# A chunked retention recurrence with a soft mixture of experts: every product of the recurrence on 64x64 quadrants

## The chip, the core and the metric

The kernel runs on one core of a Trainium2 chip, in one launch. The metric is device time in microseconds (us). A core has a matrix engine (TensorE; in the profile PE for its matmuls and PEld for the loads of their stationary operand), a vector engine (DVE), an activation engine (ACT), a general engine (POOL) and a sequencer (SP) that here issues all DMAs. Matmuls write to PSUM, everything else lies in SBUF. All data is float32, and each float32 matmul of this kernel stands in the profile as two weight loads and two matmuls; a transpose on TensorE stands as one of each.

## The reference

```python
def _attn_ref(q, k, v):                      # each 4 x 8 x 768 x 64
    gamma = 1.0 - 2.0 ** (-5.0 - np.arange(H))
    state = zeros(B, H, D, D)
    for t in range(S):
        state = gamma * state + einsum('bhd,bhe->bhde', k[:, :, t], v[:, :, t])
        y[:, :, t] = D ** -0.5 * einsum('bhd,bhde->bhe', q[:, :, t], state)

def _moe_ref(x, phi, w1, w2):                # x 3072 x 512, 8 experts with 4 slots each
    logits = x @ phi                         # 3072 x 32
    d = softmax of logits over the tokens;  c = softmax of logits over the slots
    slot_input = d.T @ x
    for e in range(8):
        slot_out[e] = np.maximum(slot_input[e] @ w1[e], 0) @ w2[e]     # 512 -> 1024 -> 512
    return c @ slot_out
```

`x` is `y` with its heads side by side. `w1` and `w2` are 16.8 MB each; q, k and v 6.3 MB each.

## The kernel before

**Steps.** A batch of 768 tokens is cut into 6 chunks of 128, so that 4 batches make 24 steps `i` (`NSTEP`). The powers of gamma are put into a scale of `v` (`load_v`, on POOL) and a scale of the result (`scale`, on DVE), so that in between the recurrence is a plain one. Eight heads are handled as four pairs `g` of two heads `r`; the head `r` of a pair lies on partitions `64r` to `64r+63`.

**One step, in the order of TensorE** (its order is the program's; the other engines are ordered by a planner):

- `scores(i + 1)`: for each pair, head and half of the chunk (`late`), k times q, 64 stationary columns on 64 rows, which is one quadrant of the array; 192 or 128 moving columns. The last 64 of these multiply with an identity that lies behind q in the tile, which gives k in its natural layout for the state (not in the last chunk of a batch). DVE multiplies all 128x128 products of a head with the mask (L205, giving `A`), ACT copies the natural k (L209).
- `inter(i)`: the state times q, on quadrants, 128 moving columns (L223), into `y`.
- every fourth step, one of three pieces of the mixture of experts for the four steps before: `logits_mm` (L277), `dispatch_p` (L310) and `dispatch_u` (L319).
- `intra(i)`: `v` times the masked `A`, all 128 rows, 64 stationary columns, 128 moving columns (L234). It also multiplies the quarter of `A` that the mask has set to zero.
- `scale(i)` on DVE reads `y` (L245).
- `state(i)`: natural k times v, all 128 rows, 64 stationary columns, 64 moving columns (L258), added up in PSUM; ACT copies it to `sst` (L260), which `inter(i + 1)` reads.
- `natural(i - 1)`: four 128x128 transposes (L266), which ACT copies (L267).

**After the 24 steps** come the last group's logits, the slot inputs, the first expert layer (`hidden`, L486), the second (L578), and the combination with `c` (L560), whose output goes to memory in twelve DMAs of 512 KB.

**DMA.** SP issues everything, in one queue. A ring of 43 tiles of 4 KB a partition holds the weights (64 loads of 512 KB) and the working tiles of the recurrence (three a step). Within the 24 steps, 31/23 weight loads a step are issued ahead of `load_v(i + 2)` and `load_kq(i + 3)`; 7 more follow at the end (`TAIL`). k and q have four tiles in turn, so `load_kq(i + 3)` waits until step `i - 1` has read its own.

Of the kernel before, what the change touches and what calls it, by code (L numbers as in the profile page):

```python
# [17 lines left out]
C = 128  # L18
# [6 lines left out]
NE = 8  # L25
# [23 lines left out]
K_MASK, K_VSC, K_YT, K_FIRST = 0, 256, 304, 400  # L49
K_ID, K_YB, K_J, K_ALL = 400, 528, 552, 556  # L50
# [8 lines left out]
def half_of(r, g):  # L59


    return r if g < NPAIR // 2 else 1 - r


def head_of(half, g):
    return 2 * g + np.where(g < NPAIR // 2, half, 1 - half)


def constants():
    g = 1.0 - 2.0 ** (-5.0 - np.arange(H, dtype=np.float64))  # L70
    p = np.arange(128)
    k = np.zeros((128, K_ALL), np.float64)

    tok = np.stack([p, (p + D) % C], axis=1)
    k[:, K_MASK:K_MASK + 256] = (p[None, None, :] >= tok[:, :, None]).reshape(128, 256)
    t = np.arange(NC)[None, :, None] * C + tok[:, np.arange(H) // 2 % 2][:, None, :].astype(np.float64)
# [11 lines left out]
def retention_soft_moe_kernel(  # L88
# [15 lines left out]
    ring = ctx.enter_context(tc.tile_pool(name="ring", bufs=NRING))  # L104
    ps = ctx.enter_context(tc.tile_pool(name="ps", bufs=1, space=PSUM))
# [3 lines left out]
    def slot():  # L109
        return ring.tile([128, 1024], F32, name="r", tag="r")  # L110

# [18 lines left out]
    mask = kt[:, K_MASK:K_MASK + 256].rearrange("p (a t) -> p a t", t=C)  # L130
# [4 lines left out]
    w1t, w2t, w2n = {}, {}, [0]  # L135
    weights = [("w1", 4 * g + j, k) for g in range(2) for k in range(NK) for j in range(4)]
    for cb, (_, w) in enumerate(BLOCKS):
        for g in range(2):
            if w == 64:
                weights += [("w2", 4 * g + 2 * j, cb) for j in range(2)]  # L140
            else:
                weights += [("w2", 4 * g + j, cb) for _ in range(NFC // FPS[w]) for j in range(4)]

    def load_weights(n):
        for _ in range(n):
            if not weights:
                return
            which, e, k = weights.pop(0)
            t = slot()
            if which == "w1":  # L150
                nc.sync.dma_start(t, w1[e, k * 128:(k + 1) * 128, :])
                w1t[e, k] = t
            else:
                n = 1024 if BLOCKS[k][1] == 64 else FPS[BLOCKS[k][1]] * BLOCKS[k][1]
                nc.sync.dma_start(t[:, 0:n], w2[w2n[0]:w2n[0] + 128 * n].rearrange("(p n) -> p n", n=n))
                w2n[0] += 128 * n
                if BLOCKS[k][1] == 64:
                    w2t[e, k], w2t[e + 1, k] = [t[:, 0:512]], [t[:, 512:1024]]
                else:
                    w2t.setdefault((e, k), []).append(t)  # L160
# [19 lines left out]
    def load_v(i):  # L180
        t = slot()
        v = t[:, 0:512].rearrange("p (h e) -> p h e", e=D)
        st[i].update(v=v, kn=t[:, 512:1024].rearrange("p (h e) -> p h e", e=D))
        nc.sync.dma_start(t[:, 0:512], v_in[i])
        nc.gpsimd.tensor_tensor(v, v, vsc[:, i % NC, :].unsqueeze(2).broadcast_to([128, H, D]), ALU.mult)  # L185


    def scores(i):
        s = st[i]
        state = i % NC < NC - 1  # L190
        A = s["A"] = slot().rearrange("p (r g t) -> p r g t", r=2, t=C)
        for hf in range(2):
            scv = sct[hf][:, :, 0:384].rearrange("p r (g n) -> p r g n", n=192)
            for gg in range(2):
                g = 2 * hf + gg
                for late in range(2):
                    for r in range(2):
                        o = (late if g % 2 == 0 else 1 - late) * D
                        kb = KB[2 * g + late]
                        n = 2 + state - late  # L200
                        nc.tensor.matmul(scv[o:o + D, r, gg, late * D:(late + n) * D],  # L201
                                         s["kq"][r * D:(r + 1) * D, kb * D:(kb + 1) * D],
                                         blocks(s["kq"], r, NB - (2 - late) * QS[g], QS[g], n),
                                         start=True, stop=True)
            nc.vector.tensor_tensor(A[:, :, 2 * hf:2 * hf + 2], scv[:, :, :, 0:C],  # L205
                                    mask.unsqueeze(1).broadcast_to([128, 2, 2, C]), ALU.mult)
            if state:
                kn = s["kn"].rearrange("p (g r) e -> p r g e", r=2)[:, :, 2 * hf:2 * hf + 2]
                nc.scalar.copy(kn, scv[:, :, :, C:C + D])  # L209
# [3 lines left out]
    def inter(i):  # L213
        s = st[i]
        y = s["y"] = [ps.tile([128, 2, C], F32, name=f"y{b}") for b in range(2)]
        if i % NC == 0:
            return
        for gl in range(2):
            for b in range(2):
                g = 2 * b + gl  # L220
                for r in range(2):
                    o = half_of(r, g) * D
                    nc.tensor.matmul(y[b][o:o + D, gl, :], sst[r * D:(r + 1) * D, g, :],  # L223
                                     blocks(s["kq"], r, NB - 2 * QS[g], QS[g], 2),
                                     start=(gl == 0), stop=False, skip_group_check=True)

    def intra(i):
        s = st[i]
        c = i % NC
        y = s["y"]  # L230
        for g in range(NPAIR):
            for r in range(2):
                o = half_of(r, g) * D
                nc.tensor.matmul(y[g // 2][o:o + D, g % 2, :], s["v"][:, 2 * g + r, :], s["A"][:, r, g, :],  # L234
                                 start=(c == 0 and g % 2 == 0), stop=True, skip_group_check=True)

    def scale(i):
        s = st[i]
        y = s["y"]
        c = i % NC  # L240
        x = slot()
        yT = s["yT"] = x[:, 0:512].rearrange("p (g t) -> p g t", t=C)
        s["xn"] = x[:, 512:1024]
        for g in range(NPAIR):
            nc.vector.scalar_tensor_tensor(yT[:, g, :], y[g // 2][:, g % 2, :], ybs[:, c, g:g + 1], ysc[:, g, :],  # L245
                                           ALU.mult, ALU.mult)

    def state(i):
        s = st[i]
        c = i % NC  # L250
        if c == NC - 1:
            return
        if c == 0:
            spsum[0] = ps.tile([128, NPAIR, D], F32, name="S")
        S_ = spsum[0]
        for g in range(NPAIR):
            for r in range(2):
                nc.tensor.matmul(S_[r * D:(r + 1) * D, g, :], s["kn"][:, 2 * g + r, :], s["v"][:, 2 * g + r, :],  # L258
                                 start=(c == 0 and g == 0), stop=True, skip_group_check=True)
        nc.scalar.copy(sst, S_)  # L260

    def natural(i):
        s = st[i]
        xp = ps.tile([128, DM], F32, name="misc")
        for g in range(NPAIR):
            nc.tensor.transpose(xp[:, g * 128:(g + 1) * 128], s["yT"][:, g, :], ident)  # L266
        (nc.vector.tensor_copy if i == NSTEP - 1 else nc.scalar.copy)(s["xn"], xp)  # L267
# [3 lines left out]
    def logits_mm(g, js):  # L271
        q = gs.setdefault(g, {})
        if "ltp" not in q:
            q["ltp"] = ps.tile([128, C], F32, name="misc") if g < NGRP - 1 else pe_[0].tile([128, C], F32, name="sm", bufs=2)
# [32 lines left out]
    def dispatch_p(g):  # L307
        q = gs[g]
        pp = ps.tile([128, 128], F32, name="misc") if g < NGRP - 1 else pe_[0].tile([128, 128], F32, name="sm", bufs=2)
# [340 lines left out]
```

## Time and profile before

| | |
|---|---|
| median of 3 runs | 171.19 us (170.9 to 173.21) |
| profiled execution: its time / its span | 172.56 us / 170.8 us |
| TensorE clock granted, mean | 0.975 |
| PE busy | 153.2 us, 2748 matmuls |
| DVE / ACT / POOL busy | 90.8 / 55.4 / 30.8 us |
| moved by DMA | 59.63 MB, 349 GB/s over the span |

The page gives the busy time of each engine, a picture of the span in 40 slices, the DMA queues, the chain of waits that ended last, and the costliest groups of instructions. Beside it the trace answers by stretch (busy time and number of instructions in a window), by group and in order of time. An engine's name with "ld", as in PEld, is the weight load of TensorE. "issue" in the chain is time in which an engine waited for nothing that the profile shows. The count of a window holds every instruction that lies in it in part.

### The profile page before, as it was taken

What the parts mean: (1) busy time and instruction counts of PE and PEld (TensorE: products, weight loads), DVE (VectorE), ACT (ScalarE), POOL (GpSimd) and SP (SyncE); (2) the same over time, 40 slices, a digit from 0 to 9 for tenths busy, and PEclk for the clock granted to TensorE, in tenths of its full rate; (3) what the DMA queues carried; (4) which work ended last, traced back from release to release, by engine and by line L of the source; (5) the groups of instructions that cost most, each with busy time, mean ns of one, the idle gap of its engine ahead of it and who ended that gap; (6) DMA issues with size and microseconds to landing.
All of it is one profiled execution on the core that took longest, in us unless ns stands there. A gap on an engine that the chain in (4) does not pass through costs nothing.

```text
span 170.8 us, 6449 instructions
## 1 busy us (share of the span) xinstructions
PE 153.2 (90%) x2748; PEld 111.0 (65%) x2748; DVE 90.8 (53%) x259; ACT 55.4 (32%) x138; POOL 30.8 (18%) x40
## 2 busy tenths in 40 slices
PE   8599996999999999999899999999999999998500
PEld 2299985778887888777668887876325466665300
DVE  1456657655686687655866589761031202653600
ACT  3114431444441544333533443343020200533300
POOL 0252222223132222222320314001300000000000
PEclk9969999999999999999999999999999999999985
DMA  5999999897999989999998898799899999999993
GB/s 190 330 404 408 405 377 343 308 378 235 386 336 351 364 321 364 343 340 337 378 355 288 271 403 317 253 338 368 291 345 421 411 406 411 407 409 410 417 419 129
DMA packets 18317, 59.63 MB, mean 349 GB/s; under 512 B 2032, under 2 KB 2416, under 8 KB 18288
## 3 DMA queue, kind: packets, MB, share of 16 engines
q1 hardware_dynamic: 18288, 59.21, 93.1%
q8 instruction: 22, 0.36, 0.8%
q14 instruction: 7, 0.06, 0.1%
HBM read 52.91 MB, written 6.29 MB: 347 GB/s over the span
## 4 chain that ended last, share of the span: by engine, by line
PE 76%; DMA 10%; DVE 4%; issue 3%; ACT 1%; SPq 1%; DVEq 0%
PE sc L201 16%; PE y L234 13%; PE misc L266 8%; PE sc L578 6%; DMA r<-in_w_dram 6%; PE y L223 5%; PE S L258 5%; PE y L486 4%; DMA kq<-in_kq_dram 4%; PE misc L277 3%; PE misc L319 3%; PE misc L486 2%; PE S L486 2%; DVE r L245 1%; PE sm L363 1%
## 5 line engine op out<-in xcount | busy, mean ns | idle before, releaser
L205 DVE TENSOR_TENSOR r<-sc,kt 128x512 f32<-128x512 f32 x48 | 31.3, 684 | 20.9 <-PE sc L201 17.4
L185 POOL TENSOR_TENSOR r<-r,kt 128x512 f32<-128x512 f32 x24 | 25.3, 1053 | 72.5 <-DMA r<-in_v_dram 60.8
L201 PE MATMUL sc<-kq 64*64 64x128 f32 (+2 forms) x768 | 31.4, 301 | 2.1 <-DMA kq<-in_kq_dram 1.9
L245 DVE SCALAR_TENSOR_TENSOR r<-y,kt,ysc 128x128 f32<-128x128 f32 x96 | 27.6, 344 | 4.0 <-PE y L234 3.6
L201 PEld LDWEIGHTS sc<-kq 64*64 64x64 f32 x768 | 25.1, 136 | 7.1 <-issue 3.0
L234 PE MATMUL y<-r 128*64 128x128 f32 x384 | 27.5, 283 | 0.5 <-issue 0.4
L234 PEld LDWEIGHTS y<-r 128*64 128x64 f32 x384 | 21.3, 139 | 8.4 <-issue 5.1
L209 ACT COPY r<-sc 128x256 f32<-128x256 f32 x40 | 14.9, 372 | 32.2 <-DVE r L205 32.2
L578 PE MATMUL sc<-r 128*32 128x128 f32 (+1 forms) x384 | 16.3, 311 | 0.8 <-DMA r<-in_w_dram 0.8
L266 PE MATMUL misc<-kt,r 128*128 128x128 f32 x96 | 15.6, 285 | 1.0 <-DVE lb L305 0.7
L267 ACT COPY r<-misc 128x512 f32<-128x512 f32 x23 | 13.5, 586 | 8.4 <-PE misc L266 6.9
L578 PEld LDWEIGHTS sc<-r 128*32 128x32 f32 x384 | 10.7, 109 | 7.1 <-issue 2.9
L258 PE MATMUL S<-r 128*64 128x64 f32 x320 | 13.4, 222 | 1.6 <-issue 1.6
L260 ACT COPY sst<-S 128x256 f32<-128x256 f32 x20 | 7.4, 372 | 19.9 <-PE S L258 19.8
L266 PEld LDWEIGHTS misc<-kt,r 128*128 128x128 f32 x96 | 10.1, 141 | 5.0 <-issue 2.1
L223 PE MATMUL y<-kq,sst 64*64 64x128 f32 x320 | 12.7, 270 | 0.0
L258 PEld LDWEIGHTS S<-r 128*64 128x64 f32 x320 | 12.3, 138 | 0.4 <-issue 0.4
L223 PEld LDWEIGHTS y<-kq,sst 64*64 64x64 f32 x320 | 10.3, 133 | 0.2 <-ACT sst L260 0.2
L486 PE MATMUL y<-r,siT 128*32 128x512 f32 x64 | 8.2, 597 | 0.0
L367 ACT CAST r<-sm 128x512 fp32r<-128x512 f32 x4 | 2.2, 587 | 13.9 <-PE sm L363 13.9
L277 PE MATMUL misc<-r,phis 128*32 128x128 f32 x160 | 5.4, 276 | 0.3 <-issue 0.3
L563 ACT COPY r<-misc 128x512 f32<-128x512 f32 x3 | 1.8, 590 | 11.4 <-PE misc L560 11.4
(114 smaller groups left out, 130.3 us busy)
## 6 DMA issues: line engine op xcount, KB each, us to landing
r<-in_w_dram SPq DMA_DIRECT2D x64, 512.0 KB, 7.5
kq<-in_kq_dram SPq DMA_DIRECT2D x20, 512.0 KB, 5.7
r<-in_v_dram SPq DMA_DIRECT2D x24, 256.0 KB, 7.1
out_dram<-r SPq DMA_DIRECT2D x12, 512.0 KB, 9.7
kq<-in_kq_dram SPq DMA_DIRECT2D x4, 544.0 KB, 6.6
kt<-in_consts_dram SPq DMA_DIRECT2D x1, 200.0 KB, 3.6
kt<-in_consts_dram SPq DMA_DIRECT2D x1, 78.0 KB, 5.9
phis<-in_phi_dram SPq DMA_DIRECT2D x1, 64.0 KB, 6.7
```

Source lines behind the costliest of these rows:

```text
L185: nc.gpsimd.tensor_tensor(v, v, vsc[:, i % NC, :].unsqueeze(2).broadcast_to([128, H, D]), ALU.mult)
L201: nc.tensor.matmul(scv[o:o + D, r, gg, late * D:(late + n) * D], s["kq"][r * D:(r + 1) * D, kb * D:(kb + 1) * D], blocks(s["kq"], r, NB - ...
L205: nc.vector.tensor_tensor(A[:, :, 2 * hf:2 * hf + 2], scv[:, :, :, 0:C], mask.unsqueeze(1).broadcast_to([128, 2, 2, C]), ALU.mult)
L209: nc.scalar.copy(kn, scv[:, :, :, C:C + D])
L223: nc.tensor.matmul(y[b][o:o + D, gl, :], sst[r * D:(r + 1) * D, g, :], blocks(s["kq"], r, NB - 2 * QS[g], QS[g], 2), start=(gl == 0), stop ...
L234: nc.tensor.matmul(y[g // 2][o:o + D, g % 2, :], s["v"][:, 2 * g + r, :], s["A"][:, r, g, :], start=(c == 0 and g % 2 == 0), stop=True, sk ...
L245: nc.vector.scalar_tensor_tensor(yT[:, g, :], y[g // 2][:, g % 2, :], ybs[:, c, g:g + 1], ysc[:, g, :], ALU.mult, ALU.mult)
L258: nc.tensor.matmul(S_[r * D:(r + 1) * D, g, :], s["kn"][:, 2 * g + r, :], s["v"][:, 2 * g + r, :], start=(c == 0 and g == 0), stop=True, s ...
L266: nc.tensor.transpose(xp[:, g * 128:(g + 1) * 128], s["yT"][:, g, :], ident)
L267: (nc.vector.tensor_copy if i == NSTEP - 1 else nc.scalar.copy)(s["xn"], xp)
L486: nc.tensor.matmul(hp[g][half][32 * j:32 * j + 32, :], siT[:, k, :], w1t[4 * g + j, k][:, half * 512:(half + 1) * 512], start=(k == 0), st ...
L578: nc.tensor.matmul(op[32 * j:32 * j + 32, :w], hT[fc // 4][:, fc % 4, 4 * g + j, :], t[:, f * w:(f + 1) * w], start=(g == 0 and fc == 0), ...
```

## The change

All products of the recurrence, `intra` and `state` too, are done on 64x64 quadrants. A head's 128x128 `A` becomes three 64x64 blocks: two triangles on the diagonal, masked with one 64x64 triangle, and a full block that needs no mask; the fourth, all zero, is neither made nor multiplied. `intra` thus has three matmuls of 64 columns a head instead of one of 128 over 128 rows, and `state` two of 64 rows instead of one of 128. DVE masks half as many elements; ACT copies the full block together with the natural k.

As one PSUM place is now added to from both row halves of the array, each of these is done in two rounds (`second`): `attend(i, 0)` holds the state's part and the first half of `intra`, `attend(i, 1)` the rest, and between them a small copy on DVE (`turn`) reads one column of `y`, so that the second round waits for the first. `emit` orders the matmuls of several lists so that each quadrant gets the same number of columns. A step is now: state of `i - 1` (second round), scores of `i + 1`, state of `i` (first round); `attend(i, 0)`; `turn`; a piece of the mixture of experts, if one is due; `natural(i - 1)`; `attend(i, 1)`; `scale(i)`.

The logits and the dispatch of the groups lie in columns of the score tiles that the scores do not use; `dispatch_u` writes four pieces of 128 columns where it wrote 512. The ring holds weights only (35 tiles), the recurrence works in 18 tiles of 2 KB a partition, and four weights are loaded as two halves into those. In the recurrence 35/21 weight loads a step are issued from step 2 on, then 4 (`TAIL`). In the tail the k/q tiles hold the hidden layer.

```diff
-TAIL = (2, 2, 1, 2)
+TAIL = (0, 2, 2, 0)
-NPRE = 31
+NPRE = 35
-NRING = 43
+NRING = 35
+NHALF = 18
+NSPLIT = 4
...
+def row_of(late, g):
+    return late if g < NPAIR // 2 else 1 - late
...
+    def emit(*lists):
+        at, todo = {}, []
+        for ls in lists:
+            for quadrant, n, fn in ls:
+                todo.append((at.get(quadrant, 0), len(todo), fn))
+                at[quadrant] = at.get(quadrant, 0) + n
+        for _, _, fn in sorted(todo, key=lambda x: x[:2]):
+            fn()
...
+    def scores_out(i):
...
+        n = (1 + state) * D
         for hf in range(2):
             scv = sct[hf][:, :, 0:384].rearrange("p r (g n) -> p r g n", n=192)
...
+            nc.vector.tensor_tensor(A[:, hf], scv[:, :, :, 0:D],
+                                    tri.unsqueeze(1).unsqueeze(1).broadcast_to([128, 2, 2, D]), ALU.mult)
+            nc.scalar.copy(Bs[hf][:, :, :, 0:n], scv[:, :, :, D:D + n])
...
+    yb = [ps.tile([128, 2, C], F32, name=f"y{b}") for b in range(2)]
+
+    def turn():
+        nc.vector.tensor_copy(small("turn", [128, 1]), yb[0][:, 1, C - 1:C])
+
+    def attend(i, second):
...
+        for g in (0, 1, 2, 3) if second else (1, 0, 3, 2):
+            for r in range(2):
+                o = half_of(r, g)
+                y = yb[g % 2][rows(o), g // 2, :]
+                first = bool(g < 2 and not second)
+                if not second and c > 0:
+                    ls.append(product(y, o, C, sst[rows(r), g, :], r, blocks(s["kq"], r, NB - 2 * QS[g], QS[g], 2),
+                                      start=first, stop=False))
+                    first = False
+                a = 1 - r if second else r
+                late = a == row_of(1, g)
+                A = s["A"][rows(a), g // 2, r, g % 2, :]
+                v = s["v"][rows(a), 2 * g + r, :]
+                if late:
+                    ls.append(product(y[:, D:C], o, D, v, a, A, start=first, stop=bool(second)))
+                else:
+                    ls.append(product(y[:, 0:D], o, D, v, a, A, start=first, stop=True))
+                    ls.append(product(y[:, D:C], o, D, v, a, s["B"][g // 2][rows(a), r, g % 2, 0:D],
+                                      start=False, stop=bool(second)))
+        return ls
...
+    def state(i, second):
...
         for g in range(NPAIR):
             for r in range(2):
+                a = 1 - r if second else r
+                late = a == row_of(1, g)
+                ls.append(product(spsum[0][rows(r), g, :], r, D,
+                                  s["B"][g // 2][rows(a), r, g % 2, (1 - late) * D:(2 - late) * D], a,
+                                  s["v"][rows(a), 2 * g + r, :], start=bool(c == 0 and not second and g == 0), stop=True))
+        if second:
+            ls.append(((1, 0), 0, lambda: nc.scalar.copy(sst, spsum[0])))
+        return ls
...
+        us = [sct[k // 2][:, k % 2, 384:512] for k in range(NK)]
...
+        for k, uk in enumerate(us):
+            for j in range(GRP):
+                nc.tensor.matmul(uk[32 * j:32 * j + 32, :], q["p"][:, 32 * j:32 * j + 32],
+                                 st[GRP * g + j]["xn"][:, k * n:(k + 1) * n],
+                                 start=True, stop=True, tile_position=(0, 32 * j))
...
+            emit(state(i - 1, 1) if i > 1 else [], [] if last else scores(i + 1), state(i, 0))
+            if not last:
+                scores_out(i + 1)
+            emit(attend(i, 0))
+            turn()
...
+        if i > 0:
+            natural(i - 1)
...
+        if i > 0:
+            emit(attend(i, 1))
+            scale(i)
```

More of the change, by code (lines that the diff above doesn't have):

```diff
@@ L138, in retention_soft_moe_kernel @@
         for g in range(2):
[L139 to L142, printed above, removed]
+            weights += [("w2", 4 * g + j, cb) for _ in range(NFC // FPS[w]) for j in range(4)]
     def load_weights(n):
@@ L190, in scores @@
         state = i % NC < NC - 1
-        A = s["A"] = slot().rearrange("p (r g t) -> p r g t", r=2, t=C)
+        ls = []
+        for g in range(NPAIR):
+            for late in range(2):
+                for r in range(2):
+                    o = row_of(late, g)
+                    kb = KB[2 * g + late]
+                    n = 2 + state - late
+                    out_ = sct[g // 2][rows(o), r, g % 2 * 192:g % 2 * 192 + n * D]
+                    ls.append(product(out_, o, n * D, s["kq"][rows(r), kb * D:(kb + 1) * D], r,
+                                      blocks(s["kq"], r, NB - (2 - late) * QS[g], QS[g], n), start=True, stop=True))
@@ L192, in scores @@
+        return ls
+    def scores_out(i):
+        s = st[i]
+        state = i % NC < NC - 1
+        A = s["A"] = half_tile().rearrange("p (f r g t) -> p f r g t", f=2, r=2, t=D)
+        Bs = s["B"] = [half_tile().rearrange("p (r g n) -> p r g n", r=2, n=2 * D) for _ in range(2)]
+        n = (1 + state) * D
         for hf in range(2):
             scv = sct[hf][:, :, 0:384].rearrange("p r (g n) -> p r g n", n=192)
[L194 to L209, printed above, removed]
-    spsum = {}
[L213 to L225, printed above, removed]
@@ new lines, in scale @@
+    def scale(i):
+        s = st[i]
+        c = i % NC
+        yT = s["yT"] = half_tile().rearrange("p (g t) -> p g t", t=C)
+        for g in (0, 2, 1, 3):
+            nc.vector.scalar_tensor_tensor(yT[:, g, :], yb[g % 2][:, g // 2, :], ybs[:, c, g:g + 1], ysc[:, g, :],
+                                           ALU.mult, ALU.mult)
+    def state(i, second):
+        s = st[i]
+        c = i % NC
+        ls = []
+        if c == NC - 1:
+            return ls
+        if c == 0 and not second:
+            spsum[0] = ps.tile([128, NPAIR, D], F32, name="S")
@@ L248, in state @@
[L248 to L260, printed above, removed]
+                a = 1 - r if second else r
@@ L316, in dispatch_u @@
         last = g == NGRP - 1
[L317 to L320 removed]
+        us = [sct[k // 2][:, k % 2, 384:512] for k in range(NK)]
+        if last:
+            u = ps.tile([128, DM], F32, name="y1")
+            us = [u]
+        n = DM // len(us)
+        for k, uk in enumerate(us):
[3 more added lines that the diff above has]
+                                 start=True, stop=True, tile_position=(0, 32 * j))
         if g == 0:
[L322 removed]
+            for hf in range(2):
+                nc.scalar.copy(acc[:, hf * 256:hf * 256 + 256].rearrange("p (r n) -> p r n", r=2), sct[hf][:, :, 384:512])
         elif last:
@@ L398, in retention_soft_moe_kernel @@
         g, ph = i // GRP, i % GRP
-        budget += NPRE / (NSTEP - 1)
-        load_weights(int(budget))
-        budget -= int(budget)
-        if not last:
-            scores(i + 1)
-        inter(i)
+        if i > 1:
+            budget += NPRE / (NSTEP - 3)
+        load_weights(int(budget + 1e-6))
+        budget -= int(budget + 1e-6)
+        if i == 0:
+            emit(state(0, 0))
+            emit(attend(0, 0))
+            turn()
+            emit(attend(0, 1), state(0, 1), scores(1))
+            scale(0)
+            scores_out(1)
+        else:
+            emit(state(i - 1, 1) if i > 1 else [], [] if last else scores(i + 1), state(i, 0))
+            if not last:
+                scores_out(i + 1)
+            emit(attend(i, 0))
+            turn()
         if i + 2 < NSTEP:
```

151 lines of the change are left out of this document (74 added, 77 removed).

## The prediction, made before the change was run

> **What bounds the kernel now.** First the page: its engines, its DMA queues, and the shares of the chain of waits.
>
> ```profile
> PE 153.2 (90%) x2748; PEld 111.0 (65%) x2748; DVE 90.8 (53%) x259; ACT 55.4 (32%) x138; POOL 30.8 (18%) x40
> q1 hardware_dynamic: 18288, 59.21, 93.1%
> q8 instruction: 22, 0.36, 0.8%
> PE 76%; DMA 10%; DVE 4%; issue 3%; ACT 1%; SPq 1%; DVEq 0%
> ```
>
> TensorE carries the chain, and the DMA engines are close behind. The third line is small and will matter: 22 transfers of instructions, 0.36 MB / 22 = 16 KB each. TensorE alone has 2748 + 2748 = 5496 instructions in the trace, 250 for each of the 22.
>
> Second, the busy time by stretch, for the recurrence and for what follows it (time and PE, PEld, DVE, ACT, POOL busy with their counts; granted clock, DMA share, GB/s):
>
> ```profile
> 8.39:110.19 101.80, 98.30 (x2057) 80.81 (x2057) 69.52 (x196) 39.87 (x105) 27.29 (x32) 0.98 0.95 345
> 110.19:170.80 60.61, 49.22 (x650) 27.98 (x649) 18.75 (x59) 13.52 (x30) 2.30 (x3) 0.96 0.95 370
> 130.00:160.00 30.00, 27.94 (x457) 17.09 (x446) 10.41 (x28) 6.66 (x12) 0.00 (x0) 1.00 1.03 410
> ```
>
> In the recurrence PE is busy 98.3 of 101.8 us; the tail of 60.6 us moves the rest of the weights and the output, at up to 410 GB/s, which I take for the full rate. The change is worth what it does to the 101.8 us.
>
> Third, one regular step in order of time (PE alone: start, length, group):
>
> ```profile
> 16.51 1.32 PE L201 MATMUL sc<-kq 64*64 64x192 f32 x32
> 17.64 0.62 PE L223 MATMUL y<-kq,sst 64*64 64x128 f32 x16
> 18.19 1.09 PE L234 MATMUL y<-r 128*64 128x128 f32 x16
> 19.12 0.63 PE L258 MATMUL S<-r 128*64 128x64 f32 x16
> 19.68 0.65 PE L266 MATMUL misc<-kt,r 128*128 128x128 f32 x4
> 20.27 0.38 PE L201 MATMUL sc<-kq 64*64 64x192 f32 x4
> ```
>
> From start to start: scores 1.13 us, state's part 0.55, `intra` 0.93, `state` 0.56, transposes 0.59, together 3.76 us, with 84 matmuls and as many weight loads: 168 instructions.
>
> Fourth, the chain in order of time, where it has no PE work:
>
> ```profile
> 23.04 0.23 PE S L258 x6
> 23.27 0.28 issue
> 23.55 0.56 PE S L258 x10
> ...
> 28.46 1.33 issue
> ...
> 73.43 0.15 issue
> ...
> 78.55 0.29 issue
> ...
> 84.84 0.45 issue
> ```
>
> The first, for one, stops in the middle of a run of like matmuls, where nothing is waited for. The stretches from one resumption to the next tell why:
>
> ```profile
> 23.54:29.77 6.23, 4.91 (x125) 4.17 (x126) 3.79 (x12) 1.42 (x4) 1.12 (x2) 1.00 0.97 351
> 73.57:78.83 5.26, 4.97 (x125) 4.32 (x125) 3.23 (x8) 1.76 (x5) 1.76 (x2) 1.00 0.95 365
> 78.83:85.28 6.45, 5.84 (x126) 4.83 (x126) 5.10 (x19) 2.54 (x9) 1.77 (x3) 1.00 0.99 359
> 92.03:97.22 5.19, 5.19 (x136) 4.42 (x128) 3.48 (x8) 2.45 (x6) 2.09 (x2) 1.00 0.76 215
> ```
>
> The first three hold 251, 250 and 252 instructions of TensorE, the number of one instruction transfer (with a few semaphore instructions it is 256). So TensorE stops because its next block of instructions has not come. As each of these stretches begins and ends with such a stop, its length is what a block takes to come when the one before is entered: 6.23, 5.26 and 6.45 us, mean 5.98, with the DMA engines at a share of 0.95 to 0.99. The old kernel uses a block in about 251 / 168 x 3.76 = 5.6 us, so it just gets by. In the fourth stretch, where the DMA share was 0.76, PE was never idle over 5.19 us: there a block took no longer than that.
>
> The Trainium skill, "Runtime: NRT & Kernel Launch", section "Instruction fetch mechanics", says that instructions come in blocks of 16 KiB, 256 instructions, the next page being fetched while the current one runs; with that the trace agrees (251, 250, 252). It also holds that fetching is hidden because the sequencer dispatches slower than blocks come; the five stops say otherwise. By that rule the result would be that of the first rival below.
>
> **The change part by part.**
>
> *Array time.* Scores stream (8 x 192 + 8 x 128) / 4 = 640 columns a quadrant in 1.13 us, 1.77 ns a column. New: scores with both `state` rounds, 640 + 256 = 896 columns, 1.59 us; `attend` first, 256 + 192 = 448, 0.79; second, 192, 0.34; transposes 0.59; one change of tiling more around them, priced at what the old change after the state's part costs (0.55 less 256 x 1.77 ns = 0.10). Sum 3.41 us against 3.76: 0.35 saved a step, 8.4 us in 24.
>
> *Instructions.* Here the change adds. The counts of the old groups:
>
> ```profile
> L234 PE MATMUL y<-r 128*64 128x128 f32 x384 | 27.5, 283 | 0.5 <-issue 0.4
> L258 PE MATMUL S<-r 128*64 128x64 f32 x320 | 13.4, 222 | 1.6 <-issue 1.6
> 104.80 1.06 PE L319 MATMUL misc<-r,p 128*32 128x512 f32 x8
> ```
>
> `intra` triples (+768), `state` doubles (+320), `dispatch_u` goes from 8 to 32 in each of five groups (+120): 1208 matmuls and as many loads, 2416 instructions. The recurrence had 2057 + 2057 = 4114; it gets 6530, or 6530 / 251 = 26.0 blocks instead of 16.4. A regular step has 132 pairs, 264 instructions, so at 3.41 us a block is used up in 3.2 us. No stretch above shows one coming that fast. So TensorE is paced by its instructions: one block lies ready, 25 are waited for.
>
> What does a block take then? Waiting should shrink with the DMA load. The recurrence moves k, q and v (20 x 512 + 4 x 544 + 24 x 256 KB), 0.34 MB of constants and 38 weights of 512 KB, 39 MB in all:
>
> ```profile
> r<-in_w_dram SPq DMA_DIRECT2D x64, 512.0 KB, 7.5
> kq<-in_kq_dram SPq DMA_DIRECT2D x20, 512.0 KB, 5.7
> r<-in_v_dram SPq DMA_DIRECT2D x24, 256.0 KB, 7.1
> kq<-in_kq_dram SPq DMA_DIRECT2D x4, 544.0 KB, 6.6
> ```
>
> Over some 130 us that is 300 GB/s, a share of 0.74 of 410. Upper end: 5.6 us, half way between the shortest and the mean under full load. Lower end: if all of the block time were waiting and shrank with the load, 5.98 x 0.74 / 0.97 = 4.5. I take 5.0, nearest to the fourth stretch with its share of 0.76. Then the recurrence ends at 8.4 + 25 x 5.0 = 133.4 us instead of 110.2: **23.2 us later**. The array's 8.4 us are inside that pace and bring nothing. At 4.5 it is +10.7, at 5.6 +38.2.
>
> *DVE and ACT*, priced by these rows:
>
> ```profile
> L205 DVE TENSOR_TENSOR r<-sc,kt 128x512 f32<-128x512 f32 x48 | 31.3, 684 | 20.9 <-PE sc L201 17.4
> L209 ACT COPY r<-sc 128x256 f32<-128x256 f32 x40 | 14.9, 372 | 32.2 <-DVE r L205 32.2
> L267 ACT COPY r<-misc 128x512 f32<-128x512 f32 x23 | 13.5, 586 | 8.4 <-PE misc L266 6.9
> L266 PE MATMUL misc<-kt,r 128*128 128x128 f32 x96 | 15.6, 285 | 1.0 <-DVE lb L305 0.7
> 142.34 0.42 DVE L541 COPY os<-sc 128x256 f32<-128x256 f32 x1 [5.36 <-PE sc L578]
> ```
>
> 48 masks of half the size fall from 684 to about 420 ns (-13 us of DVE). ACT's copies double in size: 40 x 0.586 + 8 x 0.372 = 26 us for 15. Neither engine comes near its step, so both count nothing.
>
> *New waits.* `turn` stands on DVE behind the masks of the next scores, with `scale` and the logits' reductions behind it; TensorE's second round waits for it. Its cover is `natural` (0.59 us), and it is a one-column copy: nothing while paced, and 0.1 to 0.3 us a step if the cover is gone. Logits and dispatch now share PSUM tiles with the scores, which then wait for the logits' readers; the like wait on the old shared tile cost 0.7 us in all (L305 in the L266 row), and goes. Taken as even, with 0 to 3 us as ends.
>
> *Weights.* 35/21 of 0.524 MB a step with k, q and v are 1.66 MB, 4.0 us at 410 GB/s: above the array's step but below the paced one (264 / 251 x 5.0 = 5.3 us), so this too is hidden; without the pacing it is the next limit. The four halved weights add four DMA issues. In both kernels 39 weights can lie in SBUF before the first expert layer, so the tail has the same 25 loads and the output to move: 60.6 us, taken unchanged (1.5 us either way for the doubled small DVE instructions and for halves that come late).
>
> *Sum.* Span 170.8 + 23.2 = 194.0. The profiled execution took 172.56 us in its own time, the median of the runs is 171.19; the difference put on the median gives 171.2 + 23.2 = **194.4 us**.
>
> **The rivals.** All hang on the time of a block; the change breaks even where 25 blocks take the old 101.8 us, 4.07 us each. Two per cent, about what a measurement tells from no change, is 3.4 us or 0.14 us a block.
>
> *Faster: blocks come in time.* If a block takes under about 3.9 us (or more than one is fetched ahead), the array decides: 171.2 - 8.4 = 162.8, and up to 2.5 less as the five stops (0.28 + 1.33 + 0.15 + 0.29 + 0.45) go. DMA allows it: the last v has 33 weights ahead of it, 36.6 MB, 89 us at 410 GB/s. For it speaks that waiting is partly DMA load; against it, that this same load would then be at 0.9 and more, where 5.26 was the shortest seen. 0.12, at 160 to 167.
>
> *No change: 3.94 to 4.2 us a block*, the saved load shortening the wait more than in proportion; 171. 0.08.
>
> *Array no cheaper.* That 64-column matmuls on quadrants cost as much as longer ones is spoken against by the step above (`state`: 16 of 64 columns in 0.56 us, `intra`: 16 of 128 in 0.93), and it would be inside the pace.
>
> **How the numbers follow.** Paced by instructions: 0.80, its own range 182 (4.5 us a block) to 209 (5.6). The range that holds 8 in 10 reaches down over the no-change case: 168 to 209; left out are the faster case and blocks over 5.6 us. Faster by over 2%: 0.12; within: 0.08; slower: 0.80.
>
> **What would show it.** If right: the recurrence ends near 133 us; the chain has "issue" at some 45 us (25 x 1.8) instead of 5 (3% of 170.8); about 250 instructions between its stops; instruction transfers go from 22 to about 31 or 32; the DMA share in the recurrence falls to about 0.75; ends of the tail are alike. If the array decides: few issue stops, steps of 3.4 us. It would be wrong if a block came much faster at a lower DMA load, and too low if the granted clock fell in the stops: at half clock a block lasts 6.4 us of array time.

## The result: 18 per cent slower

The kernel after took 202.2 us (median of 4 runs, 200.5 to 203.4), the kernel before 172.2 us beside it: a ratio of 1.176, 95% interval 1.161 to 1.192. The profiled execution of the kernel after took 202.39 us, with a span of 200.5 us. From the page of the kernel after: the busy times, the slices of the granted clock and of the DMA engines, the queues, and the chain's shares.

```profile
PE 160.2 (80%) x3956; PEld 119.4 (60%) x3956; DVE 85.8 (43%) x309; ACT 65.8 (33%) x147; POOL 30.6 (15%) x42
...
PEclk9999999999979969999999999999999999999985
DMA  6999999999969996965573723209319999999994
...
q1 hardware_dynamic: 18864, 59.11, 78.3%
q8 instruction: 31, 0.51, 1.1%
...
PE 35%; DVE 5%; DMA 5%; ACT 5%; issue 5%; DVEq 0%
```

TensorE has 3956 matmuls and as many weight loads, 1208 more of each, as counted ahead, and 31 transfers of instructions instead of 22. Its share of the chain fell from 76% to 35%; but this chain reaches back to 81.92 us only, so its shares can't be set beside those of before. The DMA row is not even: full in most of the first 18 slices, well below that in all but one of the next twelve, full again in the tail.

By stretch, with the columns as before. The recurrence ends where TensorE starts on the last logits, now at 138.47 us; the second and third rows are its two parts, the fourth is the tail:

```profile
8.39:138.47 130.08, 103.37 (x3258) 87.92 (x3258) 62.43 (x222) 50.21 (x115) 28.75 (x36) 0.97 0.77 284
15.45:89.54 74.09, 54.51 (x1653) 45.90 (x1652) 31.68 (x114) 26.63 (x61) 14.75 (x16) 0.95 0.96 367
89.54:138.47 48.93, 43.81 (x1435) 37.46 (x1435) 27.77 (x99) 21.02 (x49) 12.06 (x15) 1.00 0.45 142
138.47:200.50 62.03, 49.96 (x655) 28.19 (x649) 21.27 (x82) 13.18 (x30) 0.40 (x1) 0.95 0.85 333
```

The recurrence takes 28.3 us more (130.08 for 101.80), the tail 1.4 more. In the recurrence TensorE is idle for 130.08 - 103.37 = 26.7 us, where it was 3.5 us: 23.2 of the 28.3. Its busy time rises by the other 5.1 us.

Who ended TensorE's idle time in the recurrence of the kernel after (total, times, longest):

```profile
PE y L213 <- issue: 9.1, 7, 2.3
PE sc L213 <- issue: 6.1, 5, 2.4
PE sc L374 <- issue: 3.4, 1, 3.4
PE S L213 <- issue: 1.9, 4, 1.2
PE sc L213 <- ACT p L361: 1.4, 3, 0.6
PE sc L326 <- ACT h L245: 1.4, 3, 0.7
...
PE sc L326 <- issue: 0.6, 2, 0.4
```

The rows "issue" add up to 21.1 us, where the kernel before had 2.3; all others to 4.8 instead of 2.9. So the time went mostly where the forecast put it: TensorE waits for nothing but its next instructions. 20.6 of the 21.1 us lie in 17 stops, and in the trace each of these comes a multiple of 256 instructions after the first of them (semaphore instructions counted), and 1.1 to 1.6 us after the end of a transfer of instructions. Stretches from one stop to the next, or to the next block, each one block of 256 instructions (a few records are missing); the share of the DMA engines is the last column but one:

```profile
42.10:48.12 6.02, 4.00 (x128) 3.22 (x127) 1.70 (x6) 2.29 (x5) 1.57 (x2) 1.00 1.02 406
48.12:54.24 6.12, 3.67 (x128) 3.19 (x128) 1.71 (x6) 1.54 (x3) 1.04 (x1) 1.00 1.03 404
54.24:59.51 5.27, 5.27 (x125) 4.75 (x129) 1.51 (x5) 1.34 (x3) 0.56 (x1) 0.68 0.67 229
64.90:71.85 6.95, 3.32 (x127) 2.77 (x127) 2.06 (x7) 1.25 (x4) 1.04 (x1) 0.98 1.02 400
71.85:77.84 5.99, 5.58 (x126) 4.60 (x127) 2.86 (x8) 2.03 (x4) 1.04 (x1) 0.74 0.84 332
97.58:101.22 3.64, 3.37 (x128) 3.00 (x127) 1.94 (x8) 2.13 (x4) 1.04 (x1) 1.00 0.46 141
101.22:105.60 4.38, 3.81 (x128) 3.17 (x128) 1.84 (x7) 1.52 (x6) 1.04 (x1) 1.00 0.70 219
```

In the fourth row PE is busy for less than half of the 6.95 us that the block lasts. In the third and the fifth the granted clock is 0.68 and 0.74: after the two longest stops (2.4 and 3.4 us) the clock stood at half for 3.4 us each.

### The profile page after: what moved, and what is told of

It reads as the page before. It is cut to its first block, busy times and chain, and to the rows that moved or that the text cites. A ratio compares the mean times of both kernels' runs of the same rounds, so it can differ in the third digit from the quotient of the medians.

```text
span 200.5 us, 8905 instructions
## 1 busy us (share of the span) xinstructions
PE 160.2 (80%) x3956; PEld 119.4 (60%) x3956; DVE 85.8 (43%) x309; ACT 65.8 (33%) x147; POOL 30.6 (15%) x42
## 3 DMA queue, kind: packets, MB, share of 16 engines
HBM read 52.81 MB, written 6.29 MB: 295 GB/s over the span
## 4 chain that ended last, share of the span: by engine, by line
PE 35%; DVE 5%; DMA 5%; ACT 5%; issue 5%; DVEq 0%
PE sc L653 5%; DMA r<-in_w_dram 5%; PE sc L213 4%; PE y L213 4%; PE y L559 4%; PE misc L314 3%; ACT h L245 2%; PE misc L559 2%; PE S L559 2%; ACT h L316 2%; PE sc L374 2%; PE S L213 1%; DVE h L288 1%; PE sc L326 1%; PE sm L423 1%
## 5 line engine op out<-in xcount | busy, mean ns | idle before, releaser
L213 PE MATMUL sc<-kq 64*64 64x192 f32 (+2 forms) x768 | 43.2, 300 | 8.9 <-issue 6.1
L213 PE MATMUL y<-h 64*64 64x64 f32 x1152 | 36.5, 227 | 5.4 <-issue 5.0
L199 POOL TENSOR_TENSOR h<-h,kt 128x512 f32<-128x512 f32 x24 | 25.0, 1043 | 81.2 <-DMA h<-in_v_dram 64.7
L213 PEld LDWEIGHTS y<-h 64*64 64x64 f32 x1152 | 31.1, 137 | 9.4 <-issue 7.0
L288 DVE SCALAR_TENSOR_TENSOR h<-y,kt,ysc 128x128 f32<-128x128 f32 x96 | 27.4, 344 | 20.9 <-PE y L213 20.9
L245 ACT COPY h<-sc 128x512 f32<-128x512 f32 (+1 forms) x48 | 25.6, 550 | 29.8 <-DVE h L243 28.0
L213 PE MATMUL S<-h 64*64 64x64 f32 x640 | 28.8, 223 | 2.7 <-issue 1.9
L213 PEld LDWEIGHTS S<-h 64*64 64x64 f32 x640 | 25.0, 136 | 4.1 <-issue 2.4
L243 DVE TENSOR_TENSOR h<-sc,kt 128x256 f32<-128x256 f32 x48 | 19.8, 420 | 14.3 <-PE sc L213 12.8
L653 PE MATMUL sc<-r,kq 128*32 128x128 f32 (+1 forms) x352 | 16.3, 304 | 0.6 <-DMA r<-in_w_dram 0.6
```

Source lines behind the costliest of these rows:

```text
L213: return (row, o), n, lambda: nc.tensor.matmul(out_, lhsT, rhs, skip_group_check=True, **kw)
L243: nc.vector.tensor_tensor(A[:, hf], scv[:, :, :, 0:D], tri.unsqueeze(1).unsqueeze(1).broadcast_to([128, 2, 2, D]), ALU.mult)
L245: nc.scalar.copy(Bs[hf][:, :, :, 0:n], scv[:, :, :, D:D + n])
L288: nc.vector.scalar_tensor_tensor(yT[:, g, :], yb[g % 2][:, g // 2, :], ybs[:, c, g:g + 1], ysc[:, g, :], ALU.mult, ALU.mult)
L653: nc.tensor.matmul(op[32 * j:32 * j + 32, :w], hT[fc // 2][:, fc % 2, 4 * g + j, :], t[:, f * w:(f + 1) * w], start=(g == 0 and fc == 0), ...
```

## The experiments

In none of the kernels is a part of the computation left out. The runs called "no weights" (and the one that adds idle matmuls to that) load all expert weights after the recurrence, so their tails are long and only their recurrences are compared; the idle matmuls write values that the next matmul overwrites. The numbers for all of them, read in the traces as for the two kernels above (end of the recurrence; instruction blocks that TensorE used in it, counted from the first place where one block ends and the next begins, at 9 to 12 us; length of a block, which is the time of its fetch only where TensorE stops for it; TensorE's idle time put down to "issue", and to all else that the view of waits names):

| kernel | recurrence ends, us | blocks | us a block | idle: issue | idle: else |
|---|---|---|---|---|---|
| before | 110.2 | 16.0 | 6.12 | 2.3 | 2.9 |
| after | 138.5 | 25.3 | 5.10 | 21.1 | 4.8 |
| e1, after, no weights | 125.7 | 25.3 | 4.59 | 9.8 | 8.1 |
| e2, after, 264 to 232 instructions a step | 134.9 | 22.3 | 5.61 | 16.5 | 6.4 |
| e3, before, idle matmuls | 138.2 | 25.0 | 5.16 | 11.2 | 0.3 |
| e4, before, new memory | 110.8 | 16.0 | 6.29 | 4.2 | 1.3 |
| e5, after, loads in order | 138.6 | 25.3 | 5.10 | 20.6 | 4.0 |
| e6, e2 and no weights | 116.3 | 22.3 | 4.81 | 3.4 | 6.2 |
| e7, e6 with the old PSUM tile | 122.7 | 21.4 | 5.29 | 1.3 | 18.4 |
| e8, before, no weights | 104.7 | 16.0 | 5.90 | 0 | 3.1 |
| e9, e3 and no weights | 126.2 | 25.0 | 4.65 | 1.9 | 1.8 |
| e10, before, loads in order | 107.7 | 16.0 | 6.06 | 2.4 | 2.5 |

**Which half of the change does it: e3 and e4.** e3 gives the kernel before nearly as many more instructions as the change does (2304 for 2416), and nothing else of it:

```
# kernel before, in inter()
+        for n in range(24 // 4):
+            for b in range(2):
+                for r in range(2):
+                    o = half_of(r, 2 * b) * D
+                    nc.tensor.matmul(y[b][o:o + D, 0, 0:1], s["kq"][r * D:(r + 1) * D, 0:D],
+                                     s["kq"][r * D:(r + 1) * D, 0:1], start=True, stop=True, ...)
         if i % NC == 0:
             return
```

> The old kernel with 24 idle matmuls a step ahead of the state's part, one moving column each, on quadrants, into places of y that are overwritten: 48 loads and 48 matmuls a step, 2304 instructions in all, the number that the change adds (2416). Nothing else of the change. Theory: 9.2 blocks more, so the recurrence is paced by its blocks, 25.6 x 5 = 128 us instead of 101.8, and ends near 137 (130 to 143) with stops some 250 instructions apart; whole time about 198. Rival, the slowdown belongs to the quadrants and their new waits: only the array time of the idle matmuls is added, at most a quarter of 58 ns for each of the 48, 0.7 us a step: the recurrence ends at 127 or sooner.

Measured: 199.97 us in one run (span 198.1), recurrence end 138.2. That is the pace by instructions, and not the rival. A step without a stop shows what the idle matmuls cost the array itself:

```profile
17.05:21.51 4.46, 4.46 (x137) 4.05 (x133) 2.41 (x7) 1.70 (x4) 0.83 (x1) 1.00 0.89 299
```

4.46 us for 3.76, so some 24 x 0.70 = 16.8 of the 28.0 us are array work; the idle time at "issue" rises by 8.9 us (11.2 for 2.3). e3 shows that instructions that do almost nothing cost this much, but it is not a pure copy of the kernel after, which has less array work and more waiting.

e4 is the other half alone, the new working set in the kernel before:

```
-NPRE = 31
+NPRE = 35
-NRING = 43
+NRING = 35
+NHALF = 18
+NSPLIT = 4
...
-        t = slot()
-        v = t[:, 0:512].rearrange("p (h e) -> p h e", e=D)
+        t = half_tile()
+        v = st[i]["v"] = t.rearrange("p (h e) -> p h e", e=D)
```

> The other half of the change alone: products, waits and PSUM places of the old kernel, but the ring of 35 tiles for weights only, the working set in 18 tiles of 2 KB, four halved weights, the new pace of the loads and the hidden layer in the k/q tiles. Theory (instructions): TensorE's program is the old one, so it comes out like the old kernel, ratio 0.98 to 1.02; if weights are fetched earlier and faster, blocks come a little later and a few us are lost in the recurrence. Rival, the new ring and its pace cost the time (DMA full from 10 to 88 us): ratio above 1.10.

Measured: 174.8 us, ratio 1.013 (1.009 to 1.018), recurrence end 110.8. The memory is not what made the kernel slow; the recurrence on quadrants is.

**Is it the DMA load that makes a block slow: e1, e8, e9, e5.** e1 is the kernel after without weights beside the recurrence:

```
-TAIL = (0, 2, 2, 0)
+TAIL = (0, 0, 39, 0)
-ORDERED = {mybir.EngineType.PE}
-NPRE = 35
+ORDERED = {mybir.EngineType.PE, mybir.EngineType.SP}
+NPRE = 0
```

> The changed kernel with SP's DMAs in the order of the program and no weight load within the 24 steps; the 39 come after them. Only the end of the recurrence is read (138.5 us in the changed kernel); the whole gets longer, since the weights come late. Theory, TensorE waits for its blocks of instructions, and these wait behind the DMA load: all blocks come as in the lightly loaded second half of the changed kernel (about 11.5 blocks of 251 instructions in the 49.0 us from 89.54, 4.3 us each, the shortest 3.7): the recurrence ends at 9.6 + 25 x 4.1 = 112, between 105 and 117. Rival, the new waits (turn, shared PSUM tiles, DVE and ACT chains) cost it: they do not change, and the recurrence ends at 133 to 139.

Measured: recurrence end 125.7, between the two. Its rows, with the weights away and where they come in:

```profile
15.00:100.00 85.00, 75.41 (x2436) 63.97 (x2439) 46.10 (x168) 37.90 (x87) 19.15 (x21) 1.00 0.50 162
108.00:125.74 17.74, 12.85 (x410) 10.49 (x408) 9.28 (x35) 6.02 (x16) 2.77 (x5) 1.00 0.95 362
```

In 85 us TensorE used (2436 + 2439) / 256 = 19.0 blocks, 4.46 us each, at a DMA share of 0.50: blocks do come sooner. The theory gave too early an end for two reasons: a block still took 4.46 us where no weights moved, not 4.1 (9 us in 25 blocks), as other waits (8.1 us) showed under the stops; and the weights were issued from 109 us on, before the recurrence was over, and held up its last two steps. e8 and e9 close the second gap with a load that waits for the last step's k and q to be used, ahead of the weights:

```
+    nc.sync.dma_start(kqt[3][:, 0:1024], kq_in[NSTEP - 1, :, 0:1024])
     load_weights(TAIL[2])
```

> The old kernel with no weight load before the recurrence has ended. Theory: its stops (4.3 us in all at block boundaries) come from the DMA load, so they go, and nothing else changes: the recurrence ends at 104 to 107 instead of 110.2. Rival, a block takes its time whatever the DMA does: 109.5 to 111.

> The kernel before with 24 idle one-column matmuls a step (overwritten by what follows, so nothing is left out), and with all weights loaded only after the recurrence. In the run with idle matmuls and weights beside it, a regular step that met no stop took 4.46 us from transposes to transposes against 3.76 us in the kernel before, so the idle matmuls are 24 x 0.70 = 16.8 us of array work. Theory (a block of instructions comes sooner when the DMA engines have little to do): 216 instructions a step in 4.46 us use up 256 in 5.3 us, more than the 4.2 to 4.4 us that blocks took in the runs without weights, so the stops all but go (under 2 us in sum instead of 14.6) and the recurrence ends at 104.7 + 16.8 = 121.5 us (120 to 123). Rival (a block takes its 5.2 to 5.7 us whatever the load): 8.4 + 25 x 5.2 to 5.7 = 138 to 151 us, with stops as before.

e8: recurrence end 104.7, as the theory had it, with no idle time at "issue" at all, where the kernel before had 2.3 us. That is part of the 5.5 us by which it ends sooner; another 1.7 us is the clock, which stood at half for 3.41 us in the kernel before (first row) and not in e8, and no run shows that the weights caused that. e9: end 126.2, 4.7 us later than the 121.5 forecast and 3.2 past its range, but far from the rival's 138 and more. The idle at "issue" fell from e3's 11.2 to 1.9 us. Of the miss, 1.9 us are these stops, which the expectation allowed for (under 2) and did not add, and 1.7 are again 3.41 us at half clock (second row); the last 1.1 is open.

```profile
8.50:11.91 3.41, 3.41 (x44) 3.05 (x45) 1.44 (x3) 0.66 (x2) 2.19 (x5) 0.50 1.02 395
```

```profile
16.49:19.90 3.41, 3.41 (x44) 2.96 (x44) 1.20 (x4) 0.96 (x2) 0.92 (x1) 0.50 0.71 208
```

The recurrences as rows, e8, then e9, then e3:

```profile
8.39:104.71 96.32, 94.82 (x2057) 78.60 (x2049) 69.38 (x198) 40.01 (x105) 26.67 (x32) 1.00 0.56 183
```

```profile
8.39:126.22 117.83, 115.30 (x3209) 98.05 (x3209) 69.97 (x198) 40.03 (x105) 26.74 (x32) 0.99 0.46 152
```

```profile
8.39:138.24 129.85, 117.99 (x3198) 99.26 (x3189) 70.33 (x196) 40.11 (x105) 26.61 (x31) 0.97 0.79 272
```

e3 and e9 run the same instructions; the DMA share in the recurrence is 0.79 in the one and 0.46 in the other, and the recurrence 12 us shorter, 9.3 of them at "issue". e5 then asks whether it helps to spread the weights evenly:

```
-ORDERED = {mybir.EngineType.PE}
+ORDERED = {mybir.EngineType.PE, mybir.EngineType.SP}
```

> The changed kernel, with SP's DMAs in the order of the program, so that the weights come evenly (35/21 a step from step 2) instead of all before 88 us. Theory, a block of instructions waits behind the DMA queue: the same bytes spread over the recurrence; if the wait is proportional to the load, the mean block stays near 5.1 us and the recurrence ends at 135 to 141; if it grows faster than the load, it gets shorter, 126 to 134, and the whole 189 to 197. Rival, DMA load plays no part: 138 and 200 with no difference along the recurrence.

Measured: 202.85 us in one run, recurrence end 138.6 (138.5 in the kernel after). The load did become more even (first and second part of the recurrence: 0.82 and 0.73, for 0.96 and 0.45):

```profile
15.45:89.54 74.09, 59.59 (x1906) 50.35 (x1906) 35.77 (x129) 29.98 (x68) 14.69 (x16) 1.00 0.82 286
89.54:138.55 49.01, 39.76 (x1180) 33.80 (x1180) 23.14 (x85) 17.84 (x42) 9.90 (x13) 0.90 0.73 264
111.03:114.62 3.59, 3.59 (x137) 3.33 (x133) 2.57 (x8) 1.80 (x4) 1.04 (x1) 1.00 1.00 387
```

A block took 4.98 us in the first part and 5.32 in the second (3812 / 256 = 14.9 blocks and 2360 / 256 = 9.2), where the kernel after has 5.74 and 4.36: against that kernel the blocks moved with the load, and what the first part gained the second lost. (That e5's second part has the longer blocks at the lower share goes with its clock, 0.90 for 1.00: TensorE is idle for 1.0 us a block in both parts, and busy for 4.3 us a block instead of 4.0.) The end at 138.6 alone would fit the rival as well; what speaks against it is this shift along the recurrence. In this range the wait goes about in proportion to the load, and evening it out brings nothing. (The third row, a regular step without a stop, is used below.)

**What the wait depends on.** For the blocks of eight of these recurrences (before, after, e1 to e5, e9; the first of each left out) I counted in the trace how many bytes of loads had been issued and not yet begun to move when TensorE entered a block. The transfer that brings the next block begins 1.24 us after that, plus 1.38 us for each MB in waiting (171 blocks, correlation 0.87). Where TensorE then stops, the block's length is 2.55 us plus 0.96 times that delay (81 blocks, correlation 0.99):

| in waiting, MB | blocks with a stop | mean length, us |
|---|---|---|
| under 0.3 | 7 | 3.98 |
| 0.3 to 0.8 | 20 | 4.69 |
| 0.8 to 1.5 | 26 | 5.63 |
| over 1.5 | 28 | 6.35 |

Counted a few tenths of a microsecond earlier or later, the slope is 1.2 to 1.4 us a MB and the correlation 0.83 to 0.88. So a block's time goes with how much is queued when it is asked for. e5 fits: its mean in waiting is 0.84 MB a block, that of the kernel after 0.85. No run changed the queue alone, at the same load, so this is a relation read off the runs; that the load is a cause is what e1, e8 and e9 show.

**Fewer instructions: e2, a miss.** In the kernel after, the early half of each pair of blocks is multiplied in two matmuls of 64 columns; e2 lays their operands side by side and does it in one of 128:

```
-                    ls.append(product(y[:, 0:D], o, D, v, a, A, start=first, stop=True))
-                    ls.append(product(y[:, D:C], o, D, v, a, s["B"][g // 2][rows(a), r, g % 2, 0:D],
-                                      start=False, stop=bool(second)))
+                    ls.append(product(y, o, C, v, a, s["AB"][g // 2][rows(a), r, g % 2, 0:C],
+                                      start=first, stop=bool(second)))
```

> The changed kernel, with the triangle and the full block of the early half of a chunk side by side in SBUF, so that one matmul of 128 columns does what two of 64 did: 8 matmuls a step less (16 loads and 16 matmuls, 768 instructions in 24 steps), the same columns in the array, the same rounds and waits. One tile of the weight ring pays for the space (38 weights before the first expert layer instead of 39). Theory, paced by instructions: 768 / 251 = 3.06 blocks less at 4.9 us (130 us for 26) = 15 us less, 10 to 18; ratio to the old kernel about 1.09. Rival, the array or the new waits decide: no change beyond 2 us either way, ratio 1.17.

Measured: 200.8 us, ratio 1.165 (1.157 to 1.173), recurrence end 134.9: 3.6 us sooner where 15 were expected. Three blocks fewer, but each took longer:

```profile
15.00:91.00 76.00, 58.02 (x1526) 49.14 (x1525) 33.24 (x120) 28.53 (x65) 14.25 (x16) 0.93 0.96 361
91.00:134.91 43.91, 39.71 (x1179) 33.56 (x1179) 26.98 (x93) 18.74 (x44) 10.95 (x14) 1.00 0.46 147
```

In the first part 3051 instructions in 76.0 us are 6.38 us a block, against (1653 + 1652) / 256 = 12.9 blocks in 74.09, 5.74, in the kernel after, at the same DMA share of 0.96. My theory took the time of a block as given by the share. At its stops e2 had 1.65 MB in waiting, the kernel after 1.22; by the relation above (1.11 us a MB for the blocks with stops) that is 0.5 of the 0.8 us by which they differ there (6.22 and 5.41). Why its queue was longer I have not settled. In the second part few stops are left and other waits decide.

**What is under the stops: e6 and e7.** e6 is e2 and "no weights" with the gate; e7 puts logits and dispatch back into the PSUM tile of the kernel before:

```
-            q["ltp"] = sct[1][:, 1, 384:512] if g < NGRP - 1 else ...
+            q["ltp"] = ps.tile([128, C], F32, name="misc") if g < NGRP - 1 else ...
...
-        pp = sct[0][:, 0, 384:512] if g < NGRP - 1 else ...
+        pp = ps.tile([128, 128], F32, name="misc") if g < NGRP - 1 else ...
...
-        us = [sct[k // 2][:, k % 2, 384:512] for k in range(NK)]
+        u = ps.tile([128, DM], F32, name="y1" if last else "misc")
+        us = [u]
```

> No weight load before the recurrence has ended (they wait for a k/q tile that its last step reads), and the merged matmuls of e2: TensorE has 22.3 blocks to the end of the recurrence, and DMA carries k, q and v alone. Only the end of the recurrence is read. Theory A, blocks alone set the pace: 9.8 + 22.3 x 4.3 = 106, or sooner, as a step then uses a block in 3.7 us. Theory B, without the stops the new waits are next (steps of e1 without a stop: 3.8 us regular, 4.9 to 5.5 with a piece of the mixture of experts): four steps 18.5 us, the recurrence ends at 115 to 121.

> As e6, and logits, dispatch weights and dispatch products back in the PSUM tile that they had in the old kernel (shared with the transposes) instead of in the score tiles. Theory B, the sharing with the scores makes the new waits: the step after the logits falls from 5.2 to about 4.1 us and the recurrence ends 4 to 7 us sooner than in e6. Theory A: within 1 us of e6. If the transposes now wait for the logits' readers, as they did in the old kernel, up to 3 us of it come back.

e6: recurrence end 116.3, in the range of theory B. With few stops left (3.4 us) the new recurrence, here with the merged matmuls, still ends 11.6 us after the old one under the same condition (e8, 104.7). Step by step, from transposes to transposes, the five steps with a `dispatch_u` take 5.5 us longer than in e8, the other six up to 48 us, with most of the stops, 3.7, the last two 1.7, and the rest 0.7 together. Its stretch, and its largest waits on TensorE besides "issue":

```profile
8.39:116.33 107.94, 97.05 (x2855) 82.23 (x2850) 61.91 (x222) 49.92 (x115) 28.59 (x35) 1.00 0.51 163
```

```profile
PE sc L215 <- ACT p L364: 2.9, 5, 0.6
...
PE sc L329 <- ACT ab L249: 1.1, 2, 0.8
```

e7 is a miss on both sides: end 122.7, later instead of sooner. Where the waits went, and a regular step that met none:

```profile
L317 PE MATMUL misc<-kt,h 128*128 128x128 f32 x92 | 15.1, 286 | 12.6 <-DVE mrun L356 6.7 <-DVE acc L387 3.6 <-DVE lb L357 1.6
```

```profile
78.79:82.36 3.57, 3.57 (x117) 3.27 (x117) 1.98 (x6) 1.71 (x4) 0.78 (x1) 1.00 0.43 148
```

On the old tile the next transposes must wait for DVE to have read the logits and the dispatched sums: 12.6 us, of 18.4 for all waits but "issue". The expectation had this effect, but at 3 us at most. Sharing the scores' tile, as the change does, is the cheaper choice in this order of work.

The new waits that remain show best in the chain of the kernel after, at a step with logits, under little DMA load (start, length, what):

```profile
104.20 0.60 PE misc L314 x4
104.83 0.58 ACT h L316
105.41 0.37 ACT pT L349 x2
105.84 0.20 issue
106.04 0.17 DVE mrun L353
106.22 0.78 DVE h L288 x3
...
107.31 0.21 DVE cnat L397
107.54 0.32 ACT cnat L398
107.89 0.30 DVE cz L400
...
108.38 0.33 DVE h L243
...
108.80 0.57 ACT h L245
109.36 0.49 ACT h L316
109.85 0.18 ACT p L361
110.08 0.89 PE sc L213 x14
```

After the transposes at 104.20 the chain doesn't come back to TensorE for 5.3 us. In these rows each engine does one thing after the other: on DVE the mask of the next scores (L243) stands behind the reductions of the logits, on ACT the copies of the scores stand behind the mask, and behind those the copy `p`, which shares a PSUM tile with the next scores. TensorE has other work for most of that time, so it costs 0.6 us directly here, but it leaves no slack.

**The loads in order in the kernel before: e10.** The kernel before with its loads issued in the order written:

```
-ORDERED = {mybir.EngineType.PE}
+ORDERED = {mybir.EngineType.PE, mybir.EngineType.SP}
```

> The kernel before with the loads issued in the order in which they are written, so that the weights' transfers are spread more evenly over the recurrence. A candidate for a faster kernel. Theory (blocks wait on the DMA load, and the old kernel's load is at a share of 0.95 on the mean whatever the order): no difference, 170 to 173 us, recurrence end 109 to 112 us. Rival (the stops come from bursts that evening out would remove): the 4.3 us of stops go, 166 to 169 us.

Measured: 170.5 us for 171.5, ratio 0.994 (0.989 to 0.998). The gain is smaller than the rival's 166 to 169 us, and the idle at "issue" is 2.4 us as before, so its reason is not the one that I gave the rival, and it stays open. (The recurrence's end at 107.7 us is that of one execution, and a short one, with a span of 167.1 us; its clock was granted in full in the recurrence, which alone is 1.7 us against the kernel before.) It is the fastest of all kernels run here, but by 0.6% only, which is under the 2% that the forecast took for no change.

## Why the prediction was right, and where its terms were off

**The bound and the mechanism held.** The kernel after is paced by its instruction blocks: 21.1 us of idle time at "issue", 25.3 blocks of 5.10 us (25 of 5.0 forecast), 31 transfers. e3 has nearly the same number of instructions in the old recurrence and the same end, though with more array work and less waiting; e9 shows that the same instructions cost 12 us less when the DMA engines are less busy. By the rule of the Trainium skill ("Runtime: NRT & Kernel Launch", "Instruction fetch mechanics") that the cost of going from block to block is mostly hidden, the kernel would not have become slower for this reason; in this case 21.1 us were not hidden; where a block lasted 5.90 us and no weights were on the way (e8, no idle time at "issue") it holds.

**The end of the recurrence: 138.5 us, forecast 133.4.** The 5.1 us are the size of a block (25.3 x 0.10 = 2.5), the first block that is waited for, entered at 9.6 and not at 8.4 (1.2), and 25.3 blocks instead of 25 (1.4). The tail is 62.0 us, forecast 60.6 with 1.5 either way. The last 1.3 of the 7.8 us between 194.4 and 202.2 lie between span and median.

**"Load even at 0.74": wrong, though the mean was right (0.77).** The weights are not issued evenly: the planner of the kernel after has all 35 on the queue by 82 us, so the share is 0.96 until 89.5 us, with 5.74 us a block, and 0.45 afterwards, with 2870 / 256 = 11.2 blocks in 48.9 us, 4.36 each. That e5, with an even load, ends at the same time shows that the mean was a usable measure here. That a block's time follows from the share alone is what e2 refuted, so that 5.0 came so near to 5.10 is in part luck. (At the lower end of the range, 5.98 x 0.74 / 0.97 is 4.56 and not 4.5: +12.2 us instead of +10.7.)

**The array's 8.4 us: the step was mis-sized.** A regular step without a stop takes 3.59 us (e5) or 3.57 (e7, with fewer instructions), forecast 3.41, before 3.76: 0.17 to 0.19 saved, at most 4.6 us in 24 steps. The forecast that the saving brings nothing came true, but not only because of the pace: e6 against e8 shows none of it with 3.4 us of stops left, PE being busy for 97.05 us in e6 and 94.82 in e8. So it is unlikely that the faster rival's 160 to 167 us would have been reached even with blocks in time: without weights in the way, and less those 3.4 us, the new recurrence is still 8.2 us longer than the old one.

**DVE and ACT "count nothing", new waits "even": wrong.** Their busy times are small as forecast, 62.4 and 50.2 of 130 us, and the priced rows hold: the mask takes 420 ns as worked out. But the forecast weighed their load and not their order. Beside its instructions, TensorE waits for a chain through both after the logits. In e6, where the pace hides little, the five steps in which that falls make up 5.5 of the 11.6 us by which the new recurrence is behind; how much of the 5.5 is this chain, beyond the 2.9 us waited for `p`, was not separated. In the kernel after, idle time for others than "issue" is 4.8 us, 1.9 more than before; with fewer stops more of it shows (8.1 in e1). `turn`, of which 0.1 to 0.3 us a step were feared, cost TensorE's matmuls 0.3 us in all.

**"Some 45 us of issue in the chain": wrong.** It was 25 x 1.8, a block's 5.0 us less 3.2 us of array work. A block's work, with pieces of the mixture and their waits, took about 4.3 us, so a stop is 0.84 us on the mean; and the chain does not reach back to the recurrence's beginning, so the view of waits was the one to name.

**The clock.** The fear of half clock after stops came true in part: 0.68 and 0.74 in two blocks, 0.95 on the mean of the first part, 0.97 in the recurrence for 0.98 before. The two stretches at half clock, from 54.47 and from 71.53 us on, each follow 3.41 us in which PE was busy for little of the time:

```profile
51.06:54.47 3.41, 0.96 (x37) 0.72 (x32) 1.11 (x4) 0.43 (x2) 1.04 (x1) 1.00 1.03 398
68.12:71.53 3.41, 0.31 (x8) 0.04 (x2) 0.00 (x0) 0.00 (x0) 0.00 (x0) 1.00 1.02 396
```

The stop of 2.25 us before 89.54 was not followed by one. Together the two cost 3.4 us of array work, twice what the kernel before lost, but in blocks that are waited for anyway part of that is no loss.

## What to carry to other kernels

Count TensorE's instructions, weight loads too, as a resource with a rate of its own: in this kernel 256 of them per 4 to 6.4 us, the more the more loads are queued. Splitting matmuls to leave out masked blocks saves columns but adds instructions, and the kernel before already used a block in 5.6 us. Then check what lies under the bound that you found, and read not only the load of the engines beside it but the order in which each takes its work.

## What the runs showed of the hardware

The length of a block goes with the bytes of loads in waiting (3.98 us under 0.3 MB, 6.35 over 1.5 MB). In the first part of the kernel after, the transfer of the next block began 2.0 to 4.5 us after TensorE entered a block, took about 1.1 us, and TensorE went on some 1.4 us after its end; so a block is asked for about when the one before is entered, and not more than one lies ready. 24 matmuls of one column with their weight loads cost the array 0.70 us, 29 ns each. And twice the clock fell to half for 3.41 us, after TensorE had been busy for only 0.96 and 0.31 of the 3.41 us before; so a kernel that stops for its instructions can lose clock as well.
